# VectorE's order beside the late tile of a fused attention and mixture-of-experts kernel

## The chip, the cores and the metric

The kernel runs on one core of one Trainium2 chip. The metric is device time of one execution in microseconds (us), the median of the runs shown. TensorE is called PE here, VectorE DVE, ScalarE ACT, GpSimd POOL and SyncE SP, as in the profile.

## The reference

A linear attention with a decay per head makes 3072 tokens of 512 features; a router of two levels sends each to one of 16 experts; the expert is two matrix products with a ReLU between them, scaled by the router's weight.

```python
for t in range(S):                       # 4 batches, 8 heads, S = 768, D = 64
    state = gamma * state + k_t v_t^T
    y[:, :, t] = scale * q_t state
x = y as [3072, 512]
g = argmax(x @ w_group); e = argmax(x @ w_expert[g])       # 4 x 4 experts
h = np.maximum(xg[mask_e] @ w1[g, e], 0.0)                 # 512 -> 1024
ye = h @ w2[g, e]                                          # 1024 -> 512
out[tok_idx] = combined[:, None] * ye
```

## The kernel before, in words

**Stages.** Attention runs over 12 steps (up to some 104 us of the trace), and the routing of finished tokens runs beside it in batches. Then come the experts. Expert 0 is taken as two tiles: an early one of 128 tokens known from the first 16 chunks (`ua`), and a **late tile** of up to 108 tokens (`ub`), whose tokens are known only when the last batch is routed. Then comes expert 1 (`va`, up to 236 tokens), and then the other 14, from the one with most tokens to the one with fewest (`us[1:]`).

**Precision.** Each product of fp32 matrices is three products of 16-bit parts. The weights are split into a high part `wh` (ACT, L751) and a low part `wl` (DVE, L753), in 8 pieces of 128x1024 per expert. The tokens' rows are gathered by POOL (L775), transposed on PE into a PSUM tile `tpx` (L793), and split into high rows `xbh` (ACT, L795) and low rows `xbl` (DVE, L818). The hidden values are split out of PSUM into `hh` (ACT, L845) and `hl` (DVE, L848; for the early tile L1323 and L1330, since they are held back).

**The two layers of a tile.** `layers` is a generator. The first product has four groups `f2`, each two half blocks of 12 matmuls (L841); it yields after every half block. The second product of the late tile is `narrow`: 8 steps `k` of 12 matmuls (L947), with a yield after each. So the late tile's loop over `i` has 16 turns, 0 to 7 in the first product, 8 to 15 in the second. What is written into the loop at turn `i` is queued, on whatever engine it runs, behind what the generator queued before that yield. The order on every engine is that of the program: nothing is moved by a scheduler.

**What the late tile carries beside it.** On DVE: the ranking of the experts by their number of tokens (`order`, 9 steps, L597 to L626), which ends in the table `ord` that SP reads to choose the next experts' weights; `own_counts` (L583, L585), which makes `ocols`, the numbers of columns in expert 1's two tiles; six low pieces of expert 1's weights; and `counts` (L639 to L645), which makes `cols`, the same numbers for the later experts. On PE, `shape` reads such a number into a register of PE's queue (L806, a load that waits for DVE) and sets a matmul shape with it (L807): for `ocols` behind the late tile's steps k=1 and k=2, for `cols` behind the second group f2 of expert 1 and the third. On SP: two reads of `ord`, the lists of two experts (L768), and the loads of the next expert's weights (L725), each of which waits for a low piece that frees its buffer.

**Ahead of it**, the last batch's routing chooses experts (DVE to L403), PE makes the ranks (L436, L438), and DVE turns them into the late tile's token numbers (L555 and L567, with matmuls L563 between). Half blocks of the early tile are laid between these steps by `first(n)`.

Of the kernel before, what the change touches and what calls it, by code (L numbers as in the profile page):

```python
# [106 lines left out]
class Kernel:  # L107
# [1098 lines left out]
    def run(self):  # L1206
        tc, nc = self.tc, self.nc
        with ExitStack() as ctx:
# [18 lines left out]
            us = [dict(at=((j + 1) % 2, 0), W=(PW[-1:] + WIDTH)[j], pool=wpool[(j + 1) % 2]) for j in range(NS + 1)]  # L1227
            va = us[0]
# [4 lines left out]
            def pick(j):  # L1233
                self.picked(us[j], j - 1)

            def cols(j, i):
                return self.cols[0:1, i, j - 1:j] if j else self.own[:, i:i + 1]

            def first(n):

                for _ in range(n):
                    next(self.first, None)
# [65 lines left out]
            late.append(self.late_entries(5, self.oh[:, 0:BM, 0:1]))  # L1308
            self.route_steps(99, True)
            assert not self.steps  # L1310
            first(3)
            self.wsplit(va, 2, low=False)
            next(route)
            while next(route) != "late":
# [8 lines left out]
                nc.vector.scalar_tensor_tensor(*h)  # L1323
            for _ in route:
                pass
            first(2)
            p, y = self.at
            ent = self.entries(5, *self.chosen(y, self.yp))
            self.spreads.append((self.marks(p, self.yp), ent))
# [2 lines left out]
            nc.gpsimd.memset(self.xg[1], 0.0)  # L1332
            self.wsplit(va, 3, low=False)
            self.steps.append(self.order())
            self.route_steps(5)
            for i, k in enumerate(self.first):
                if i == 0:
                    self.wsplit(va, 4, low=False)
# [5 lines left out]
                if i == 3:  # L1344
# [3 lines left out]
                    self.nc.vector.tensor_copy(ub["mt"][:, 0, 1:2], self.final[:, 0, 1, 1:2])  # L1348
                    va["mt"] = self.final[:, 1]
                    self.gather(va)  # L1350
            self.route_steps(99)
            assert not self.steps
            pick(1)
            pick(2)
            for u in us[1:3]:
                self.listed(u)
            self.own_counts()
            self.wsplit(va, 0, high=False)
            ub["wh"], ub["wl"] = ua["wh"], ua["wl"]
            self.gather(us[1])  # L1360
            for i, k in enumerate(self.layers(ub)):
                if i in (1, 3):
                    self.wsplit(va, 6 + i // 2, low=False)
                if i in (8, 12):
                    self.xtrans(va, ("sta", "big")[i // 4 - 2], (i // 4 - 2,))
                if i in (3, 7, 12, 13, 14):
                    low = (3, 7, 12, 13, 14).index(i) + 1
                    self.wsplit(va, low, high=False)
                    if low % 2:
                        self.wload(us[1], low // 2)  # L1370
                if i in (9, 10):
                    self.shape(va, 0, i - 9, cols(0, i - 9))
                if i == 15:
                    self.counts()
# [83 lines left out]
```

## Time and profile before

| what | us |
|---|---|
| median of 3 runs (lowest, highest) | 406.8 (406.68, 407.85) |
| the profiled execution, its own time | 405.67 |
| its span, first to last instruction | 403.9 |
| PE busy, share of the span | 389.8, 97% |
| DVE busy, share of the span | 295.3, 73% |
| ACT busy, share of the span | 223.0, 55% |
| POOL busy, share of the span | 166.8, 41% |

The span is 1.8 us shorter than the execution's own time, which also holds what lies before the first and behind the last instruction. Busy shares are averages over stages with different limits, so the profile has to be read by stretches: which engine has idle time in a stretch, and what that idle time ends with. A matmul's row lasts longer than its distance to the next one, since matmuls are pipelined; time lost by PE is read from starts.

### The profile page before, as it was taken

The page shows a single profiled execution, that of the slowest core. Times are in us where ns is not written, and L with a number is a line of the kernel's source. Part 1 is how long each engine was busy: PE and PEld are TensorE (multiplying, and loading weights), DVE is VectorE, ACT ScalarE, POOL GpSimd, SP SyncE. Part 2 cuts the span into 40 slices and gives each one's busy share as a digit, 9 for nine tenths or more (in the row PEclk, how much of TensorE's full clock was granted, in tenths as well). Part 3 has the DMA queues.
Part 4 walks back from the last instruction along what each step waited for, and adds up shares of the span by engine and source line. Part 5 has one row for each costly group of instructions (what it writes and reads, how often), then busy time and mean ns, then how long its engine had stood idle before and what let it go on. Part 6 is the DMA issues. An engine that isn't in the chain of part 4 may idle for free.

```text
span 403.9 us, 13857 instructions
## 1 busy us (share of the span) xinstructions
PE 389.8 (97%) x5809; PEld 324.4 (80%) x5841; DVE 295.3 (73%) x483; ACT 223.0 (55%) x340; POOL 166.8 (41%) x172
## 2 busy tenths in 40 slices
PE   9999999999998999999999999999999999999992
PEld 5789888888858878586978888797887978879792
DVE  4575876868798879886758686776878769788620
ACT  3224434544652765565566666676666767667520
POOL 4542769659585106131416234260522505232001
PEclk9999999999999999999999999999999999999997
DMA  7999999988816897887868787979789897887001
GB/s 254 356 346 346 317 355 292 355 283 290 288 69 208 304 363 263 264 262 246 252 228 267 258 298 262 299 276 320 260 282 330 274 325 268 256 333 278 11 32 36
DMA packets 38643, 107.13 MB, mean 265 GB/s; under 512 B 12020, under 2 KB 12148, under 8 KB 31156
## 3 DMA queue, kind: packets, MB, share of 16 engines
q1 hardware_dynamic: 28752, 92.52, 67.0%
q0 software_dynamic: 9536, 12.63, 8.9%
q10 hardware_dynamic: 292, 1.08, 0.8%
q8 instruction: 47, 0.77, 0.7%
q14 instruction: 16, 0.13, 0.1%
HBM read 94.18 MB, written 13.20 MB: 266 GB/s over the span
## 4 chain that ended last, share of the span: by engine, by line
PE 46%; issue 36%; POOL 10%; DVE 4%; ACT 1%; DMA 1%; POOLq 0%; SPq 0%; ACTq 0%; DVEq 0%
PE hps L841 12%; POOL out L999 6%; PE op L299 5%; PE yps L875 5%; PE sh L235 5%; POOL xg L775 4%; PE op L286 3%; PE yps L922 3%; PE sh L345 2%; PE stp L261 2%; PE yps L925 2%; PE sh L319 1%; PE sh L220 1%; PE log L332 1%; PE tpx L793 1%
## 5 line engine op out<-in xcount | busy, mean ns | idle before, releaser
L753 DVE TENSOR_TENSOR wl<-wf,wh 128x1024 bf16<-128x1024 f32 x120 | 145.1, 1220 | 36.9 <-ACT wh L751 33.0
L751 ACT ACTIVATE wh<-wf 128x1024 f16<-128x1024 f32 (+1 forms) x136 | 133.6, 1001 | 0.1
L841 PE MATMUL hps<-xbl,wh 128*128 128x128 f16 (+16 forms) x544 | 128.4, 249 | 0.7 <-issue 0.5
L841 PE MATMUL hps<-xbh,wh 128*128 128x0 bf16 x544 | 125.9, 241 | 0.3 <-issue 0.3
L841 PE MATMUL hps<-xbh,wl 128*128 128x0 bf16 x544 | 125.9, 241 | 0.2 <-issue 0.2
L999 POOL DMA_INDIRECT out<-yo,mt x30 | 39.1, 1303 | 159.0 <-ACT yo L981 121.1
L841 PEld LDWEIGHTS <-wh 128*128 128x128 f16 x1088 | 94.9, 98 | 1.5 <-issue 0.9
L925 PEld LDWEIGHTS <-wh 128*128 128x128 f16 x768 | 47.1, 97 | 22.9
L845 ACT ACTIVATE hh<-hps 128x256 bf16<-128x256 f32 (+16 forms) x68 | 34.1, 503 | 43.6 <-PE hps L841 41.6
L775 POOL DMA_INDIRECT xg<-xd,mt x30 | 51.8, 1727 | 13.1 <-issue 5.2
L841 PEld LDWEIGHTS <-wl 128*128 128x128 bf16 x544 | 53.1, 98 | 1.6 <-issue 0.9
L247 DVE TENSOR_TENSOR pf<-sh,tri 128x512 f32<-128x512 f32 x48 | 30.6, 685 | 22.7 <-PE op L299 8.3
L795 ACT ACTIVATE xbh<-tpx 128x512 bf16<-128x512 f32 (+14 forms) x32 | 16.7, 523 | 45.9 <-PE tpx L793 45.9
L848 DVE SCALAR_TENSOR_TENSOR hl<-hps,hh 128x216 f16<-128x216 f32 (+15 forms) x64 | 36.6, 574 | 4.2 <-ACT hh L845 3.7
L922 PE MATMUL yps<-wh,hh 128*128 128x512 f16 x96 | 36.4, 379 | 0.0
L922 PE MATMUL yps<-wh,hl 128*128 128x512 f16 x96 | 36.4, 379 | 0.0
L922 PE MATMUL yps<-wl,hh 128*128 128x512 bf16 x96 | 36.3, 378 | 0.0
L818 DVE TENSOR_TENSOR xbl<-tpx,xbh 128x512 f16<-128x512 f32 (+14 forms) x32 | 19.1, 597 | 20.0 <-ACT xbh L795 20.0
L925 PEld LDWEIGHTS <-wl 128*128 128x128 bf16 x384 | 24.2, 97 | 11.4
L192 POOL TENSOR_TENSOR vs<-lv,cst 128x512 f32<-128x512 f32 x24 | 24.6, 1043 | 14.9 <-DMA lv<-qkv 9.9
L925 PE MATMUL yps<-hl,wh 128*128 128x108 f16 (+11 forms) x384 | 29.1, 198 | 0.0
L925 PE MATMUL yps<-hh,wh 128*128 128x0 bf16 x384 | 26.6, 190 | 0.0
(194 smaller groups left out, 599.1 us busy)
## 6 DMA issues: line engine op xcount, KB each, us to landing
wf<-w2p SPq DMA_DIRECT2D x29, 1024.0 KB
wf<-w1p SPq DMA_DIRECT2D x28, 1024.0 KB
lq<-qkv SPq DMA_DIRECT2D x24, 256.0 KB
lk<-qkv SPq DMA_DIRECT2D x24, 256.0 KB
lv<-qkv SPq DMA_DIRECT2D x24, 256.0 KB
xd<-xr SPq DMA_DIRECT2D x22, 256.0 KB
wf<-w1p SPq DMA_DIRECT2D x16, 256.0 KB
wf<-w2p SPq DMA_DIRECT2D x8, 256.0 KB
```

The lines of the kernel that those rows point to most:

```text
L192: self.nc.gpsimd.tensor_tensor(o, v, g, ALU.mult)
L235: nc.tensor.matmul(self.sh[2 * u + par][64 * half:64 * half + 64, cs], kT[rs, ks:ks + 64], qT[rs, cs], start=True, stop=True, skip_group_c ...
L247: nc.vector.tensor_tensor(o, sc, tri, ALU.mult)
L751: nc.scalar.activation(u["wh"][i][:, cs], u["wf"][i][:, cs], AF.Copy)
L753: (eng or nc.vector).tensor_tensor(u["wl"][i][:, cs], u["wf"][i][:, cs], u["wh"][i][:, cs], ALU.subtract)
L775: nc.gpsimd.indirect_dma_start(out=xg[0:r, i, :], out_offset=None, in_=self.xd[0:n, :], in_offset=bass.IndirectOffsetOnAxis(ap=mt[0:r, i, ...
L841: nc.tensor.matmul(o, l[:, k, fs], m, start=(n == 0), stop=(n == 11), skip_group_check=True)
L845: nc.scalar.activation(hh[:, f, 0:W], hv[:, :, 0:W], AF.Relu)
L848: nc.vector.scalar_tensor_tensor(*rest)
L922: nc.tensor.matmul(big, h[:, k, 0:P], w[k], start=(n == 0), stop=(n == 23))
L925: nc.tensor.matmul(o, w[k][:, d * P:d * P + P], m, start=(n == 0 and d == 0), stop=(n == 23), skip_group_check=True,)
L999: s = nc.gpsimd.indirect_dma_start(out=self.out, out_offset=bass.IndirectOffsetOnAxis(ap=mt[0:r, i, 0:1].bitcast(U32), axis=0), in_=yo[0:r ...
```

## The change

DVE's work beside the late tile is put in another order, and one half block of the early tile is moved ahead of the ranks. No instruction is added or removed.

```diff
-            first(3)
+            first(4)
             self.wsplit(va, 2, low=False)
...
-            first(2)
+            first(1)
...
             self.steps.append(self.order())
-            self.route_steps(5)
+            self.route_steps(3)
...
-            self.route_steps(99)
-            assert not self.steps
-            pick(1)
-            pick(2)
-            for u in us[1:3]:
-                self.listed(u)
-            self.own_counts()
-            self.wsplit(va, 0, high=False)
+            self.route_steps(2)
             ub["wh"], ub["wl"] = ua["wh"], ua["wl"]
-            self.gather(us[1])
             for i, k in enumerate(self.layers(ub)):
...
-                if i in (3, 7, 12, 13, 14):
-                    low = (3, 7, 12, 13, 14).index(i) + 1
+                if i == 1:
+                    self.wsplit(va, 0, high=False)
+                if i == 3:
+                    self.route_steps(2)
+                if i == 7:
+                    self.route_steps(99)
+                    assert not self.steps
+                    pick(1)
+                    pick(2)
+                    for u in us[1:3]:
+                        self.listed(u)
+                    self.own_counts()
+                if i == 10:
+                    self.gather(us[1])
+                if i in (7, 12, 13, 14, 15):
+                    low = (7, 12, 13, 14, 15).index(i) + 1
                     self.wsplit(va, low, high=False)
```

On DVE, from the ranking's fourth step on, before (the number behind a name is its buffer; hh_2385 and hps_2387, 2417, 2448, 2475 are the late tile's, wl_1931 is expert 1's first two low pieces):

```order
L607 TENSOR_TENSOR gt_2262<-key_2258 128x256
L612 TENSOR_REDUCE pos_2264<-gt_2262 128x16
L818 TENSOR_TENSOR xbl_2303<-tpx_2304,xbh_2302 128x4x108
L529 TENSOR_TENSOR lists_129<-lists_129,tally_2322 128x160
L534 SCALAR_TENSOR_TENSOR final_2025<-lists_129 128x32
L535 TENSOR_REDUCE final_2025<-lists_129 128x32
L1348 COPY mt_2192<-final_2025 128x1
L615 TENSOR_TENSOR eq_2341<-pos_2264,rest_94 128x256
L620 TENSOR_TENSOR eqk_2343<-eq_2341,rest_94 128x256
L623 TENSOR_REDUCE ordf_2345<-eqk_2343 128x16
L626 CAST ord_2347<-ordf_2345 128x16
L583 TENSOR_TENSOR ofc_2374<-nb_2137,rest_94 1x2
```

On DVE, the same stretch now:

```order
L818 TENSOR_TENSOR xbl_2299<-tpx_2300,xbh_2298 128x4x108
L529 TENSOR_TENSOR lists_129<-lists_129,tally_2318 128x160
L534 SCALAR_TENSOR_TENSOR final_2025<-lists_129 128x32
L535 TENSOR_REDUCE final_2025<-lists_129 128x32
L1348 COPY mt_2205<-final_2025 128x1
L607 TENSOR_TENSOR gt_2337<-key_2258 128x256
L612 TENSOR_REDUCE pos_2339<-gt_2337 128x16
L848 SCALAR_TENSOR_TENSOR hl_2342<-hps_2343,hh_2341 128x2x108
L753 TENSOR_TENSOR wl_1931<-wf_1752,wh_1930 128x1024
L848 SCALAR_TENSOR_TENSOR hl_2342<-hps_2374,hh_2341 128x2x108
L615 TENSOR_TENSOR eq_2402<-pos_2339,rest_94 128x256
L620 TENSOR_TENSOR eqk_2404<-eq_2402,rest_94 128x256
```

The late tile's low rows (L818) stand ahead of the ranking, and the low parts of h (L848) come between its steps.

On DVE, the rest of the late tile, before (wl_2129 and wl_2274 are expert 1's low pieces 2 to 5, xbl_2518 its low rows):

```order
L585 TENSOR_SCALAR ocols_2373<-ofc_2374 1x1 x2
L753 TENSOR_TENSOR wl_1931<-wf_1752,wh_1930 128x1024
L848 SCALAR_TENSOR_TENSOR hl_2386<-hps_2387,hh_2385 128x2x108
L848 SCALAR_TENSOR_TENSOR hl_2386<-hps_2417,hh_2385 128x2x108
L753 TENSOR_TENSOR wl_1931<-wf_1752,wh_1930 128x1024
L848 SCALAR_TENSOR_TENSOR hl_2386<-hps_2448,hh_2385 128x2x108
L848 SCALAR_TENSOR_TENSOR hl_2386<-hps_2475,hh_2385 128x2x108
L753 TENSOR_TENSOR wl_2129<-wf_1813,wh_2128 128x1024
L818 TENSOR_TENSOR xbl_2518<-tpx_2519,xbh_2517 128x4x128
L818 TENSOR_TENSOR xbl_2518<-tpx_2600,xbh_2517 128x4x108
L753 TENSOR_TENSOR wl_2129<-wf_1813,wh_2128 128x1024
L753 TENSOR_TENSOR wl_2274<-wf_2011,wh_2273 128x1024 x2
```

On DVE, the rest of the late tile now:

```order
L848 SCALAR_TENSOR_TENSOR hl_2342<-hps_2406,hh_2341 128x2x108
L848 SCALAR_TENSOR_TENSOR hl_2342<-hps_2433,hh_2341 128x2x108
L623 TENSOR_REDUCE ordf_2460<-eqk_2404 128x16
L626 CAST ord_2462<-ordf_2460 128x16
L583 TENSOR_TENSOR ofc_2489<-nb_2150,rest_94 1x2
L585 TENSOR_SCALAR ocols_2488<-ofc_2489 1x1 x2
L753 TENSOR_TENSOR wl_1931<-wf_1752,wh_1930 128x1024
L818 TENSOR_TENSOR xbl_2511<-tpx_2512,xbh_2510 128x4x128
L818 TENSOR_TENSOR xbl_2511<-tpx_2599,xbh_2510 128x4x108
L753 TENSOR_TENSOR wl_2142<-wf_1813,wh_2141 128x1024 x2
L753 TENSOR_TENSOR wl_2270<-wf_2011,wh_2269 128x1024 x2
L639 TENSOR_TENSOR eqc_2651<-eq_2402,cnt_2256 128x256
```

The order of experts and `ocols` (L623 to L585) stand behind all four low parts of h, and four low pieces instead of three stand between expert 1's last low rows and `counts` (L639, which before follows the last row shown). On PE, POOL and SP the order is the same as before, but for the one half block on PE.

## Rows read from the trace of the kernel before

**Rows 1.** Busy time by stretches: us, then busy time (and instructions) of PE, PEld, DVE, ACT, POOL

```profile
134.42:390.00 255.58, 255.58 (x3110) 209.36 (x3136) 197.92 (x233) 162.91 (x224) 81.58 (x53) 1.00 0.77 264
```

**Rows 2.** Timeline of PE: start us, us, what [idle before <-releaser]

```profile
106.49 0.22 PE L841 MATMUL hps<-xbh,wl 128*128 128x0 bf16 x1
107.05 0.20 PE L436 MATMUL log<-oh,stri 128*128 128x80 bf16 x1 [0.34 <-ACT ex L409]
...
115.05 0.50 PE L793 MATMUL tpx<-ident,xg 108*128 108x108 f32 x3 [0.21 <-DVE hl L1330]
...
116.77 0.72 PE L522 MATMUL tally<-yT,hot 128*128 128x160 bf16 x8
...
117.59 0.20 PE L841 MATMUL hps<-xbh,wl 128*128 128x0 bf16 x1
118.00 0.30 PE L841 MATMUL hps<-xbl,wh 128*128 128x108 f16 x3 [0.21 <-DVE xbl L818]
...
120.65 0.20 PE L841 MATMUL hps<-xbh,wh 128*128 128x0 bf16 x1 [0.27 <-issue]
...
121.39 0.21 PE L841 MATMUL hps<-xbl,wh 128*128 128x108 f16 x1 [0.50 <-issue]
...
125.10 0.28 PE L947 MATMUL yps<-hh,wh 128*128 128x0 bf16 x3 [0.23 <-issue]
...
134.52 0.26 PE L841 MATMUL hps<-xbl,wh 128*128 128x236 f16 x1
```

**Rows 3.** Timeline of DVE around the late tile

```profile
112.02 2.04 DVE L494 TENSOR_TENSOR yT<-rest,tile 128x128 bf16<-128x128 f32 x1
...
114.58 0.41 DVE L1330 SCALAR_TENSOR_TENSOR hl<-hps,hh 128x256 f16<-128x256 f32 x1
...
115.45 1.53 DVE L607 TENSOR_TENSOR gt<-key 128x256 f32<-128x256 f32 x1
...
117.35 0.59 DVE L818 TENSOR_TENSOR xbl<-tpx,xbh 128x432 f16<-128x432 f32 x1
117.86 0.31 DVE L529 TENSOR_TENSOR lists<-lists,tally 128x160 f32<-128x160 f32 x1
...
118.69 0.42 DVE L615 TENSOR_TENSOR eq<-pos,rest 128x256 f32<-128x256 f32 x1
...
120.66 1.20 DVE L753 TENSOR_TENSOR wl<-wf,wh 128x1024 bf16<-128x1024 f32 x1
121.79 0.65 DVE L848 SCALAR_TENSOR_TENSOR hl<-hps,hh 128x216 f16<-128x216 f32 x2
...
127.76 3.48 DVE L753 TENSOR_TENSOR wl<-wf,wh 128x1024 bf16<-128x1024 f32 x3
131.16 0.41 DVE L639 TENSOR_TENSOR eqc<-eq,cnt 128x256 f32<-128x256 f32 x1
...
132.28 0.17 DVE L645 TENSOR_SCALAR cols<-cols 128x14 int32<-128x14 int32 x1
```

**Rows 4.** Timeline of POOL beside these

```profile
112.61 1.28 POOL L501 TENSOR_TENSOR yT<-yT,pc 128x640 bf16<-128x640 bf16 x1
...
115.43 1.27 POOL L501 TENSOR_TENSOR yT<-yT,pc 128x640 bf16<-128x640 bf16 x1
```

**Rows 5.** Timeline of ACT and of SP's queue

```profile
115.67 0.53 ACT L795 ACTIVATE xbh<-tpx 128x432 bf16<-128x432 f32 x1 [1.47 <-PE tpx L793]
...
121.56 0.35 ACT L845 ACTIVATE hh<-hps 128x216 bf16<-128x216 f32 x1 [1.03 <-remote]
...
124.39 5.07 SPq L725 DMA_DIRECT2D wf<-w1p  x2
```

**Rows 6.** Tile ocols, and line 806 at 132 to 134: ns min/median/max, first and last start us

```profile
L806 PEldq TENSOR_LOAD <-ocols x2: 302/306/311, 123.2 to 124.2; - x2
...
L806 PEldq TENSOR_LOAD <-cols x1: 299/299/299, 132.9 to 132.9; - x1
```

**Rows 7.** Timeline of PE's weight loads, where the shape from cols is set

```profile
133.68 0.06 PEld L807 MOVE_SHAPE   x1
```

## The prediction

> **What bounds the kernel now.** First the busy time by stretches [rows 1]: from 134.42 us, where expert 1's third group begins, to 390, PE is busy 255.58 of 255.58 us. Nothing that another engine does there can end earlier than PE. So the change is worth what it moves the start of that stretch, the matmul at 134.52 [rows 2], and nothing else, as long as the later stretch stays closed. Second, the timeline of PE before it [rows 2], read for its idle marks. There are five that bear on this change: 0.34 us before the ranks (waiting for ACT's `ex`), 0.21 before the late tile's transposes (waiting for DVE's held-back `hl`, L1330), 0.21 before the late tile's first product with low rows (waiting for L818), 0.27 and 0.50 at 120.65 and 121.39 ("issue": the profile shows no wait). Third, the timelines of DVE [rows 3] and POOL [rows 4], to see what DVE does just ahead of each of these waits. Fourth, PE's own reads of shapes [rows 6], since they wait for DVE and everything on PE's queue stands behind them. The gap at 125.10 [rows 2] belongs to them: the second read of `ocols` starts at 124.2 [rows 6] and takes 0.30, and the register steps behind it some 0.6 more, which is known from the third read, of `cols`: it starts at 132.9 [rows 6] and its shape is set from 133.68 to 133.74 [rows 7], 0.84 in all.
>
> **Part 1, the ranks half a block later.** The four half blocks ahead of the ranks now hold the matmuls that filled PE's time after the token numbers. Between the starts at 106.49 and 107.05 [rows 2] PE does nothing but a matmul of 0.055 us (128 columns, the first group's pitch), so 0.5 is lost. Twelve such matmuls are 0.65 us, so the ranks come some 0.15 later, the token numbers (L567) with them, and PE is 0.5 ahead behind them. That lead ends at the transposes at 115.05, which wait for L1330 at 114.58 to 114.99 [rows 2, 3]: PE only waits there longer. Is L1330 then 0.15 later? By DVE's rows alone, yes, since DVE has no idle from L567 to it: the sum has +0.15. But L494 ahead of it lasts 2.04 [rows 3] and ends at 114.06, just behind POOL's L501, 112.61 to 113.89 [rows 4]. The Trainium skill says (SBUF — State Buffer, Who interferes with whom) that a DVE instruction with two SBUF inputs and a GpSimd instruction that reads SBUF exclude each other, and the first to start holds the port to its end; by that L494 ends with L501 whenever it starts, and the term would be 0. The sum takes 0, since 114.06 follows 113.89 by 0.17, and L607 shows the same: 115.45 to 116.98 beside the second L501, 115.43 to 116.70 [rows 3, 4]. Bounds: 0 and +0.15.
>
> **Part 2, the low rows ahead of the ranking.** Now L818 waits for L607 (1.53) and L612 and starts at 117.35. The high rows are ready at 115.67 + 0.53 = 116.20 [rows 5]. With nothing ahead of it, L818 runs from 116.26 to about 116.85; were it held by L501 to 116.70, to 117.3. Both are before 117.59, where PE first lacks low rows [rows 2]. The step from 117.59 to 118.00 falls to the pitch of 0.04: **-0.37**.
>
> **Part 3, what is late instead.** The tally's matmuls end at 116.77 + 0.72 = 117.49 [rows 2], so L529 starts at 117.5 instead of 117.86, and the four instructions up to L1348 end at 118.69 - 0.35 = 118.35 [rows 3]. From there DVE does, in order: L607 and L612 at 0.42 each, the duration of L615 of the same size, since no L501 runs now (0.84); one low part of h (0.33, half of the 0.65 at 121.79); a low piece (1.13, from 120.66 to 121.79); a low part (0.33); L615 and L620; two low parts (0.65); L623 to L585. L615 to L585 took 120.66 - 118.69 = 1.97. The sum is 5.25, so `ocols` is there at **123.6**, 2.9 later than now.
>
> PE reads it at 123.2 [rows 6], and with part 2 and without the two issue gaps it would come 0.37 + 0.77 earlier, at 122.1. So it waits, and steps k=2 to k=7 stand behind that read. The read starts 0.4 later than now, and so do the shapes, step k=3 (125.10), the transposes of expert 1's second tile, its low rows and the start of expert 1: **+0.4** where now nothing is lost. What PE gains before is given back here, whether the issue gaps vanish or not, unless they make `ocols` later (below).
>
> Behind expert 1's low rows DVE has four low pieces instead of three. Now L753 x3 and `counts` run from 127.76 to 132.28 + 0.17 = 132.45; then 0.4 + 1.13 later, at 133.98. PE's read of `cols` now starts at 132.9, 0.45 behind it; then it starts at 133.98 and the first matmul of group three 0.84 + 0.06 later, at 134.88, against 134.52: +0.36. Counted along PE instead, with the waits between 125.10 and 134.52 unchanged, it is +0.4. Two ways, nearly one number: **+0.4** at 134.52.
>
> **Part 4, at nothing.** The table `ord` is ready 2.9 later, so SP's two lists and its first weight load move from 124.39 to 127.3 [rows 5], and POOL's gathers of expert `us[1]`, which wait for those lists, by as much; nothing on SP or POOL changes places with them. Cover: ACT takes that load's data first at about 133.1 now, 8.7 after its issue; 5.8 are left for 1 MB. The gathered rows are transposed at about 141. Were this cover gone, ACT's split and the `hh` behind it would wait, and PE's second product at 139. The low pieces 1 to 3 are finished over 3 us before expert 1's groups use them. The scatter of the late tile's rows (POOL) stands behind those gathers and is waited for by none.
>
> **Sum:** -0.5 (gone at the transposes) and -0.37 on PE (given back at the read of `ocols`), and +0.4 from that read: 405.67 + 0.4 = 406.1 in the profiled execution, which is 1.1 under the median of the runs. On the median, 406.8 + 0.4 = **407.2**. A change of 0.3% (1.2 us) is what a measurement of this kernel can tell from none.
>
> **Rivals.**
> *The late part of h (slower).* The gaps at 120.65 and 121.39 are unexplained, and ACT's second `hh` of the late tile starts only at 121.56, 1.03 idle before it [rows 5]. The sum lets it start at 120.2 with the gaps. DVE now stands behind it with its low part, and behind that with the whole ranking. It decides from 120.65, when the first low piece is done. If that stall stays where it is, 0.37 earlier, `hh` ends at 121.54 and DVE goes on with 0.33, then L615 and L620 (0.92), 0.65, and 1.05: 124.5, which is 0.9 later than in the sum. The end is +1.3: **408.1**. For it: the second `hh` was late although DVE and ACT were not in its way, so this change doesn't remove its cause. Against: PE's pace into that place changes, and nothing ties a gap to it. Chance 0.27.
> *PE is not held (faster).* If the read of `ocols` is no wait, because DVE is through by about 122.2 (it would be if L494 took not 2.04 but about what L501's hold leaves out, and the transposes and the tally came earlier by what DVE gains), then the 0.37 and the 0.77 are kept, 1.14 in all, and the read of `cols` comes as early as it must: **405.6** to 405.7. For it: L494 is late by chance of POOL's order. Against: that order is not changed, and the transposes can gain no more than PE's own lead of 0.5 and the 0.21 there, half of the 1.4 that is wanted. Chance 0.15.
> *It is all hidden.* The added wait at `ocols` equals what PE gained, within 0.2: 406.8. This falls in the forecast's range. Chance 0.1 of the forecast's 0.58.
>
> **How the numbers follow.** Forecast 0.58 (406.5 to 407.7, with the +0.15 of part 1 and the half microsecond between runs), the slower rival 0.27 (407.9 to 408.5), the faster 0.15 (405.2 to 405.9). 0.3% is 405.6 and 408.0. Half of the faster rival's range lies under 405.6, and a closed PE stretch that fits better adds a little: 0.13. Slower takes most of the second case and the forecast's upper tail: 0.27. Same: 0.60. The range reaches to both rivals' middle: 405.8 to 408.5.
>
> **What would show it.** Right: L607 at about 0.42 and behind L1348; L818 done before 117.3 and no idle mark before the first product with `xbl`; `ocols` at 123.6, PE's read of it there, with an idle stretch of PE before k=2; group three of expert 1 at 134.9. Wrong: PE's read of `ocols` earlier than 122.5 (the faster rival), or a second low part of h later than 121.2 (the slower one), or idle marks of PE behind 135, which would mean that part 4's cover is gone.

## The result, and the profile after

The changed kernel takes 409.63 us (median of 7 runs) against 406.8 (7 runs): a ratio of 1.0068, 95% interval 1.0040 to 1.0095, so it is slower by some 2.8 us (1.6 to 3.9 by the interval). The forecast was 407.2, its range ended at 408.5. In the tables below the medians are over all runs, while the ratios leave out the few executions that ran in a slower state, the profiled one of e17 among them. The profiled execution of the changed kernel took 406.89 (span 405.2) and is the shortest of the seven; in it the attention part ended 0.87 us earlier than in the profile of before (DVE's choice of experts, L403, at 105.57 and at 106.44). So places in the two traces are compared by their distance from a common point: the start of the late tile's transposes (L793), 115.05 before [rows 2] and 114.24 after. From there to expert 1's third group it is 134.52 - 115.05 = 19.47 us before and 135.60 - 114.24 = 21.36 after: 1.9 more. That is inside the interval; what the medians differ by beyond it stands in no trace (see e1).

Timeline of PE after the change (start us, us, what, idle before it and its releaser), the rows that answer to [rows 2]:

```profile
114.24 0.56 PE L793 MATMUL tpx<-ident,xg 108*128 108x108 f32 x4 [0.89 <-DVE cnt L597]
...
118.43 0.20 PE L841 MATMUL hps<-xbh,wl 128*128 128x0 bf16 x1
...
119.88 0.20 PE L841 MATMUL hps<-xbh,wh 128*128 128x0 bf16 x1 [0.42 <-issue]
...
120.61 0.20 PE L841 MATMUL hps<-xbh,wl 128*128 128x0 bf16 x1 [0.41 <-issue]
...
121.33 0.21 PE L841 MATMUL hps<-xbh,wh 128*128 128x0 bf16 x1 [0.34 <-issue]
...
125.34 0.31 PE L947 MATMUL yps<-hh,wh 128*128 128x0 bf16 x4 [1.44 <-DVE ocols L585]
...
126.30 0.31 PE L947 MATMUL yps<-hh,wh 128*128 128x0 bf16 x4 [0.30 <-issue]
...
135.60 0.26 PE L841 MATMUL hps<-xbl,wh 128*128 128x236 f16 x1 [1.01 <-DVE hl L848]
```

The idle mark before the first product with low rows is gone, as forecast. The issue gaps are not: there are three now, 1.17 us of idle time, where there were two with 0.77. Then come two waits that the kernel before does not have: 1.44 us for `ocols` at step k=2, and 1.01 before group three. The second is written to DVE's L848; it ends with `cols`, as the reads show: the first of them starts at 134.6, just behind L644 (134.40 to 134.57 in DVE's timeline below), which makes the first row of `cols`.

Tile `ocols`, and line 806 at 133 to 137 (ns min/median/max, first and last start):

```profile
L806 PEldq TENSOR_LOAD <-ocols x2: 304/305/306, 124.4 to 125.4; - x2
```

```profile
L806 PEldq TENSOR_LOAD <-cols x2: 300/302/305, 134.6 to 136.2; - x2
```

One wait between groups of expert 1, for ACT's `yT` (L953), became shorter; it is 1.16 in the first of these rows, from PE before, and 0.25 in the second, from PE after:

```profile
131.86 0.65 PE L994 MATMUL tpy<-ident,yT 128*108 128x128 f32 x4 [1.16 <-ACT yT L953]
```

```profile
131.76 0.65 PE L994 MATMUL tpy<-ident,yT 128*108 128x128 f32 x4 [0.25 <-ACT yT L953]
```

Timeline of DVE after the change, which answers to [rows 3]:

```profile
111.12 2.03 DVE L494 TENSOR_TENSOR yT<-rest,tile 128x128 bf16<-128x128 f32 x1
...
115.40 0.61 DVE L818 TENSOR_TENSOR xbl<-tpx,xbh 128x432 f16<-128x432 f32 x1 [0.88 <-ACT xbh L795]
...
117.53 0.41 DVE L607 TENSOR_TENSOR gt<-key 128x256 f32<-128x256 f32 x1
...
118.61 1.22 DVE L753 TENSOR_TENSOR wl<-wf,wh 128x1024 bf16<-128x1024 f32 x1
121.78 0.38 DVE L848 SCALAR_TENSOR_TENSOR hl<-hps,hh 128x216 f16<-128x216 f32 x1 [1.96 <-ACT hh L845]
...
124.26 0.20 DVE L585 TENSOR_SCALAR ocols<-ofc 1x1 int32<-1x1 f32 x2
...
128.96 4.62 DVE L753 TENSOR_TENSOR wl<-wf,wh 128x1024 bf16<-128x1024 f32 x4
133.50 0.42 DVE L639 TENSOR_TENSOR eqc<-eq,cnt 128x256 f32<-128x256 f32 x1
...
134.40 0.17 DVE L644 SCALAR_TENSOR_TENSOR cols<-num,rest 128x14 int32<-128x14 f32 x1
134.61 0.20 DVE L645 TENSOR_SCALAR cols<-cols 128x14 int32<-128x14 int32 x1
```

POOL's L501 beside L494, which answers to [rows 4]:

```profile
111.71 1.28 POOL L501 TENSOR_TENSOR yT<-yT,pc 128x640 bf16<-128x640 bf16 x1
```

DVE sits idle for 1.96 us ahead of the second low part of h, with the ranking and `ocols` behind it. It waits for ACT's second `hh`, and ACT's row names PE as what it waits for; the timeline of ACT, which answers to [rows 5]:

```profile
117.72 0.35 ACT L845 ACTIVATE hh<-hps 128x216 bf16<-128x216 f32 x1 [0.90 <-PE hps L841]
...
121.39 0.35 ACT L845 ACTIVATE hh<-hps 128x216 bf16<-128x216 f32 x1 [2.38 <-PE hps L841]
```

The second `hh` starts 3.67 behind the first; before it was 121.56 - 119.24 = 2.32. The rows of before that this rests on, from ACT and from PE:

```profile
119.24 0.35 ACT L845 ACTIVATE hh<-hps 128x216 bf16<-128x216 f32 x1 [1.58 <-PE hps L841]
```

```profile
119.64 0.20 PE L841 MATMUL hps<-xbh,wl 128*128 128x0 bf16 x1
```

This matmul at 119.64, and the one at 118.43 after the change, is the 48th of the late tile, the last that the second `hh` needs. So by PE's rows the second `hh` comes 1.92 us behind its matmuls before and 2.96 after, and each time just behind the start that ends the last issue gap (121.39 before, 121.33 after; 0.05 to 0.17 us behind it in all ten profiles with gaps). In a profile without gaps (e15) it is 0.44. The idle time of the gaps lies behind these matmuls, so the rows do not show what holds the second `hh`; gaps and late `hh` only come together.

Behind group three the expert stretch is closed as it was (windows; the columns of [rows 1]), 254.40 busy of 254.40 us:

```profile
135.60:390.00 254.40, 254.40 (x3097) 208.31 (x3125) 197.41 (x233) 161.97 (x223) 82.00 (x53) 1.00 0.78 268
```

So the 1.9 us are lost between the late tile's transposes and group three, where PE waits at two reads of shapes. That was the place the prediction named. What was open is how much each costs, and why the second `hh` came still later.

### The profile page after: what moved, and what is told of

It is laid out like the page before. It is cut to its first block, busy times and chain, and to the rows that moved or that the text cites. A ratio compares the mean times of both kernels' runs of the same rounds, so it can differ in the third digit from the quotient of the medians.

```text
span 405.2 us, 13857 instructions
## 1 busy us (share of the span) xinstructions
PE 390.8 (96%) x5809; PEld 325.0 (80%) x5841; DVE 293.3 (72%) x483; ACT 223.2 (55%) x340; POOL 166.2 (41%) x172
## 4 chain that ended last, share of the span: by engine, by line
PE 47%; issue 35%; POOL 10%; DVE 5%; ACT 1%; POOLq 0%; DVEq 0%; ACTq 0%
PE hps L841 11%; POOL out L999 6%; PE yps L875 5%; PE op L299 5%; PE sh L235 5%; POOL xg L775 4%; PE op L286 3%; PE sh L345 3%; PE yps L922 3%; PE stp L261 2%; PE yps L925 2%; DVE wl L753 1%; PE log L332 1%; PE sh L319 1%; PE sh L220 1%
## 5 line engine op out<-in xcount | busy, mean ns | idle before, releaser
L753 DVE TENSOR_TENSOR wl<-wf,wh 128x1024 bf16<-128x1024 f32 x120 | 145.1, 1220 | 35.7 <-ACT wh L751 34.5
L848 DVE SCALAR_TENSOR_TENSOR hl<-hps,hh 128x216 f16<-128x216 f32 (+15 forms) x64 | 36.7, 574 | 6.0 <-ACT hh L845 5.6
L818 DVE TENSOR_TENSOR xbl<-tpx,xbh 128x512 f16<-128x512 f32 (+14 forms) x32 | 19.1, 597 | 22.0 <-ACT xbh L795 22.0
```

The source lines that it names most:

```text
L753: (eng or nc.vector).tensor_tensor(u["wl"][i][:, cs], u["wf"][i][:, cs], u["wh"][i][:, cs], ALU.subtract)
L848: nc.vector.scalar_tensor_tensor(*rest)
```

## The experiments

Each set of runs was taken on one chip, with runs of the kernel before beside it; the sets e1 to e18 came to five different chips (the chip of the first result is not on record). That turned out to matter: **in some sets PE has the issue gaps beside the late tile in every profile, in others in none.** Below, "chips with the gaps" stands for the chips of such sets; no chip was used for two sets, so a chip and the time of its set are not told apart.

The first table gives the times. The ratio and its interval are those on record; the ratio is not the quotient of the two medians and differs from it by up to 0.2%. The kernel before against itself (e9) gives 1.0009, with 0.27% to either side. So differences of 0.2 to 0.3% are at the edge of what can be told, and such readings below rest on the distances in the traces too.

| run | median, us | before in its set | ratio to before (95%) | issue gaps |
|---|---|---|---|---|
| e1 the change | 409.07 | 407.14 | 1.0064 (1.0034, 1.0094) | yes |
| e2 change, `ocols` early | 406.92 | 407.14 | 1.0016 (0.9991, 1.0040) | yes |
| e3 before, ranks alone | 406.90 | 407.14 | 1.0014 (0.9986, 1.0041) | yes |
| e4 before, low rows alone | 406.60 | 407.14 | 1.0002 (0.9970, 1.0033) | yes |
| e5 change, `ocols` and `cols` early | 404.40 | 405.15 | 0.9981 (0.9952, 1.0010) | no |
| e6 before, low rows, `cols` early | 404.39 | 405.15 | 0.9972 (0.9945, 0.9999) | no |
| e7 change, gather later | 406.59 | 405.15 | 1.0030 (0.9995, 1.0064) | no |
| e8 change, fixed shape | 407.17 | 405.15 | 1.0055 (1.0026, 1.0085) | no |
| e9 before | 407.39 | 406.87 | 1.0009 (0.9982, 1.0036) | yes |
| e10 the change | 408.44 | 406.87 | 1.0044 (1.0016, 1.0073) | yes |
| e11 before, `ocols` late | 408.00 | 406.87 | 1.0016 (0.9992, 1.0040) | yes |
| e12 before, low pieces shifted | 407.27 | 406.87 | 1.0007 (0.9975, 1.0038) | yes |
| e13 as e5 | 404.18 | 405.56 | 0.9974 (0.9948, 0.9999) | no |
| e14 as e6 | 404.80 | 405.56 | 0.9981 (0.9958, 1.0004) | no |
| e15 the change | 405.80 | 405.56 | 1.0024 (0.9996, 1.0051) | no |
| e16 as e12 | 406.30 | 405.56 | 1.0023 (0.9996, 1.0050) | no |
| e17 as e5 | 404.73 | 405.82 | 0.9960 (0.9929, 0.9990) | no |
| e18 before, one run | 404.37 | 405.82 | | no |

The second table gives distances on PE in the profiled executions, from the late tile's transposes (T) to its second product (Y), to expert 1's first matmul (E) and to its third group (G). The distances are free of where the attention part happened to end.

| profile | gaps | T to Y | Y to E | E to G | T to G |
|---|---|---|---|---|---|
| before | yes | 7.70 | 5.21 | 6.56 | 19.47 |
| the change | yes | 8.04 | 6.88 | 6.44 | 21.36 |
| e10 the change | yes | 8.10 | 7.02 | 6.44 | 21.56 |
| e2 `ocols` early | yes | 8.12 | 5.22 | 6.34 | 19.68 |
| e4 low rows alone | yes | 8.30 | 5.25 | 5.22 | 18.77 |
| e18 before | no | 7.16 | 6.09 | 5.22 | 18.47 |
| e15 the change | no | 6.22 | 7.32 | 6.36 | 19.90 |
| e16 low pieces shifted | no | 6.22 | 7.30 | 6.35 | 19.87 |
| e13 `ocols`, `cols` early | no | 6.22 | 6.89 | 4.79 | 17.90 |

**e1, the change again.**

> The changed kernel once more, for a second profile and more times. The theory: the loss is made in the stretch from the late tile's first product to expert 1's third group, by two waits of PE that the kernel before does not have: the read of ocols (1.44 us idle in the first profile of the change) and the read of cols (1.01). It expects both again within 0.3, ACT's second hh of the late tile again at 121 or later, PE closed from group three on, and 409.6 in the median. The rival, that the first profile's waits belong to that one execution (which was the shortest of seven) and the others lose their time elsewhere, expects under 0.7 at either read and idle marks of PE in another stretch.

T to G is 21.48; 1.48 us idle at `ocols`, 0.97 before group three, the second `hh` 3.79 behind the first. The theory's waits are there again. This set also has the mean granted clock of PE for each run. Six of the twelve runs of the change are under 0.993 (median 409.65 us, the others 408.31), and five of the 33 of the kernel before that the ratio uses (408.02, the others 406.51). Among the runs at 0.993 or more the change loses 1.8 us, and in the set of e10 1.6 (408.17 against 406.60), near the 1.9 to 2.0 of the distances. So most of the loss stands where the clock is the same. That more of the change's runs have a lower clock can account for the rest of its median; why they have it is not shown.

**e2, `ocols` alone early.** Now DVE makes it where it is idle, before the late tile.

```diff
             self.route_steps(3)
+            self.own_counts()
...
                         self.listed(u)
-                    self.own_counts()
```

> The change, with own_counts alone put back ahead of the late tile, so that ocols is ready at about 118 while ranking, low rows and low pieces stay as the change has them. The theory (PE waits at ocols because it stands behind the late second hh): PE's 1.44 us of idle time before step k=2 go, expert 1's rows and with them cols come as much earlier, and the time falls by 1.2 to 1.5 to about 408.2; what is left over the kernel before is the wait at cols, with four low pieces ahead of it. First rival (cols is bound by DVE's sum of work alone, not by PE's rows): the wait at ocols goes but the one at cols grows by as much, 409.5. Second rival (the ranks' half block or something outside the late tile costs the time): no idle at ocols and no gain, 409.6.

Timeline of PE:

```profile
123.92 0.32 PE L947 MATMUL yps<-hh,wh 128*128 128x0 bf16 x4 [0.24 <-issue]
...
133.13 0.26 PE L841 MATMUL hps<-xbl,wh 128*128 128x236 f16 x1 [1.39 <-DVE hl L848]
```

The wait at `ocols` is gone, Y to E is back at 5.22, and T to G at 19.68. The time falls from 409.07 to 406.92 in the same set, by more than the theory said: nearly the whole loss goes with this one read (T to G 21.48 to 19.68, before 19.47). The three issue gaps and the late second `hh` are unchanged. So against the kernel before, which has two gaps, the third one and the later `hh` cost little by themselves; they cost through what stands behind them on DVE. What the gaps cost against none this run does not tell: the kernel before has 19.47 with them and 18.47 without (e18).

**e3, ranks alone** (the two `first` lines of the change, on the kernel before).

> The kernel before with only the first part of the change: the ranks half a block later. The theory, as the prediction had it: 0.5 us are gained at the ranks and lost again at the late tile's transposes, which wait for the held-back low part of h: 406.8, within 0.2. The rival that the change's loss comes from here: 409 or more. A second rival (the token numbers come 0.15 later and everything behind them): 407.0.

T to G is 19.49, and the transposes wait 0.96 where they waited 0.21: the half microsecond gained at the ranks is lost there, as forecast.

**e4, low rows alone** (`route_steps(5)` to `route_steps(3)`, on the kernel before).

> The kernel before with only the second part: the late tile's low rows ahead of the last half of the ranking, which still ends ahead of the late tile, as do ocols and the first low pieces. The theory: PE's idle mark of 0.21 before the first product with low rows goes (0.37 from start to start), ocols is late by under 0.3 and is waited for by none, so 406.4 to 406.8. The rival that PE's pace at the late tile's issue gaps sets the end, whatever comes before: 406.8. The rival that putting the low rows first is itself what costs the time: 408 or more.

The first idle mark is gone, but T to Y is 8.30 against 7.70: the issue gaps are three, as in the change, and take more than the low rows give. T to G is nevertheless 18.77, because the wait of 1.16 that the kernel before has between groups of expert 1, for ACT's `yT` (L953), is not there. `ocols` stands 0.54 later behind L403 (under 0.3 was expected), and none waits for it. In the median no difference can be told.

**e5 and e6, both reads freed.** e5 is e2 with `counts` ahead of the four low pieces; e6 is e4 with `counts` ahead of the last of three.

```diff
+                    if i == 12:
+                        self.counts()
                     self.wsplit(va, low, high=False)
...
-                if i == 15:
-                    self.counts()
```

> The change with own_counts ahead of the late tile, and with counts (which makes cols) ahead of the first of the four low pieces instead of behind the fourth. The theory (what is left of the loss is PE's wait at cols, 1.39 us idle before group three in the run with own_counts early, and it comes from four low pieces ahead of counts): the idle mark before group three goes, group three stands about 27.0 behind the last choice of experts (L403) instead of 28.3, and the time falls to 405.4 to 405.8, under the kernel before. The rival (PE is then held by the late tile's second hh or by expert 1's h instead, since the four low pieces still stand between them on DVE): a new wait of 0.7 or more before group three or four, 406.5 or more.

> The kernel before with the low rows ahead of the ranking and counts one low piece earlier. The theory, by which the end is set by PE's two reads: the idle mark of 0.25 before group three in the run with the low rows alone goes (0.4 from start to start), group three stands 27.1 behind L403 instead of 27.5, 406.0 to 406.3. The rival that something else of PE holds it there: 406.6, as with the low rows alone.

No idle mark is left before group three in either (T to G 17.83 and 18.41), and both come out under the kernel before, though e5's interval includes no difference. But this set's profiles show no issue gaps at all, and the second `hh` 1.2 behind the first, although e6 has the same work in the same order as e4 up to `counts`. So DVE's order does not by itself make the gaps; the changed kernel itself has none in e15.

**e7 and e8, what the gaps hang on.** e7 moves `self.gather(va)` into the late tile's turn 5; e8 takes out the line that sets the late tile's shape, so that its matmuls run over all 108 columns.

> The change with POOL's gather of expert 1's rows issued half a product later, behind the late tile's sixth half block; the rows are transposed later by that, so the time itself is not comparable. It asks what PE's issue gaps of the late tile (three, 1.2 us idle in all) and the late second hh hang on. If on the gather's transfers: the gaps move with it, by 2 us or more, or go, and the second hh starts within 1.5 of the first plus the weight split. If on PE's own pace: gaps and second hh stand where they do in the change, 3.7 behind the first hh.

> The change without the shape that PE sets for the late tile, so that its matmuls run over all 108 columns. If PE's issue gaps and the late second hh hang on the dynamic shape, the gaps go and the second hh comes 1.5 us or more earlier; then ocols comes 1 us earlier, PE's wait there falls from 1.4 to about 0.4 and the time by about 1, less what the wider matmuls cost (at most 0.01 each, some 2 us over 192). If not: the gaps stay within 0.5 of 1.2 us in all.

Both ran in the set without gaps, so neither can tell: inconclusive. They do show that the change's second wait needs no gaps: 1.39 and 1.26 idle before group three, though there the gathered rows of expert 1 are late too (1.62 and 1.66 us of waiting for them). e8 has no wait at `ocols` and still loses 0.55%, part of which its wider matmuls take (T to Y 6.85 against 6.22).

**e9 and e10, both kernels beside each other.**

> The kernel before once more. PE's issue gaps beside the late tile (1.0 us idle or more, with the second hh 2.3 to 3.8 behind the first) stand in the six profiles taken so far in the first two sets, and in none of the four of the third set. If they belong to the set of executions (the chip they ran on) and not to the kernel, this profile has them or not as its neighbours here have. Without them the theory expects PE at the late tile to be held by the gathered rows of expert 1 (an idle mark before the transposes of step k=0) and group three about 27.5 behind L403; with them 28.1. The rival, that the gaps are the kernel's: as in the first profile, 0.27 and 0.50.

> The changed kernel beside the one before, on the same chip. The first theory (ocols stands behind the late second hh, so that the whole loss hangs on PE's issue gaps): where the gaps are absent, ocols is at 0.9 us earlier against L403, its read waits under 0.5, and the loss falls to under 1 us. The second theory (two waits of DVE's making, the second of them at cols behind four low pieces, which needs no issue gap): the idle mark before group three is 1.0 to 1.4 and the loss stays 1.5 to 2.5 whether the gaps are there or not.

This chip has the gaps, with the kernel before too. T to G is 19.62 for the kernel before and 21.56 for the change: a loss of 1.9, and 1.8 by the ratio, as the second theory says for such a chip. What the first says of a chip without gaps is answered by e15. The waits of the change in PE's timeline:

```profile
126.12 0.31 PE L947 MATMUL yps<-hh,wh 128*128 128x0 bf16 x4 [1.59 <-DVE ocols L585]
...
136.38 0.26 PE L841 MATMUL hps<-xbl,wh 128*128 128x236 f16 x1 [1.01 <-DVE hl L848]
```

**e11, the mirror of e2:** the kernel before, with `own_counts` alone moved to the late tile's turn 7.

> The kernel before with own_counts alone moved behind the late tile's four low parts of h; ranking, low rows and low pieces as before. DVE then makes ocols at about 124.4 in the time of the first profile (123.51 + 0.65 + 0.3) instead of 120.7. The theory: PE's second read of late shapes waits for it, 0.5 to 1.2 us idle at step k=2, and with three low pieces the wait at cols does not follow in full: 0.4 to 1.0 us slower than before. The rival (PE has slack there, from expert 1's gathered rows): no more than 0.2.

PE waits 1.13 us for `ocols` at step k=2, and T to G is 21.76, 2.1 over e9. In the median it is 1.1 us, by the ratio 0.65, and the interval includes no difference. The profile shows a second loss that the theory had not: 0.81 us before expert 1's first matmul, for its low rows. And the issue gaps are three (two in the kernel before), with no other change of order ahead of them. What makes two or three of them is open.

**e12 and e16, the low pieces' places alone.**

```diff
-            self.wsplit(va, 0, high=False)
...
-                if i in (3, 7, 12, 13, 14):
+                if i == 1:
+                    self.wsplit(va, 0, high=False)
+                if i in (7, 12, 13, 14, 15):
```

> The kernel before with only the positions of expert 1's low pieces taken from the change: the first one behind the late tile's first half of f2=0, four instead of three between expert 1's low rows and counts. Ranking, low rows and ocols as before. The theory (the second wait, at cols, is one low piece of 1.13 us on DVE's chain): an idle mark of 0.7 to 1.3 before group three, 0.6 to 1.1 slower than before. The rival (what delays cols in the change is PE's late arrival alone): no idle mark there, within 0.2 of before.

> The kernel before with only the low pieces' positions of the change. The theory: cols is made 1.1 later on DVE. Where PE waits 1.2 us or more for ACT's yT ahead of group three, as in the kernel before on chips with gaps, that wait covers it and the time is that of before within 0.2%; where it doesn't, an idle mark of 0.7 to 1.3 before group three and 0.2 to 0.3% over before.

With gaps (e12) the time is that of before, 1.0007; its profiled execution had PE at a lower clock for three microseconds (last section), so its distances from T on are not used. Behind that stretch the expected idle mark before group three is there (1.25 us), but the time that should have followed from it (0.6 to 1.1 more) is not: the wait for ACT's `yT`, 1.16 in the kernel before, is gone in its place. Without gaps (e16) it loses 0.23%, as much as the whole change beside it (e15, 0.24%), though either interval just reaches no difference. The timelines of DVE and of PE in e16:

```profile
129.47 4.62 DVE L753 TENSOR_TENSOR wl<-wf,wh 128x1024 bf16<-128x1024 f32 x4
```

```profile
136.02 0.26 PE L841 MATMUL hps<-xbl,wh 128*128 128x236 f16 x1 [1.39 <-DVE hl L848]
```

Four pieces, and the read waits.

**e13 to e18, the rest.**

> The change with own_counts ahead of the late tile and counts ahead of the four low pieces, on another chip if it comes so. The theory (the two waits of PE at ocols and cols are the whole loss): no idle mark over 0.4 at either read, group three 26.4 to 27.2 behind L403, and no slower than the kernel before, 0.1 to 0.3% under it, with PE's issue gaps or without. The rival (what was gained belongs to the chip without the gaps): with gaps 0.2% or more over the kernel before.

> The kernel before with the low rows ahead of the ranking and counts one low piece earlier. The theory: no idle mark at the read of cols, group three 27.1 to 27.3 behind L403, 0.1 to 0.3% under the kernel before, with the gaps or without. The rival: with gaps no different from before.

> The changed kernel. With PE's issue gaps: as in its three profiles, idle 1.4 to 1.6 at the read of ocols and 1.0 at cols, group three 30.0 to 30.3 behind L403, 0.4 to 0.7% over before. Without them: no wait at ocols (PE waits for the gathered rows one step before), 1.2 to 1.4 at cols, group three 28.5 to 29, 0.2 to 0.4% over before.

> The change with own_counts ahead of the late tile and counts ahead of the four low pieces. With PE's issue gaps the theory expects group three about 27.1 behind L403 (28.31 in the run with own_counts early, less its wait at cols of 1.2) and 0.1 to 0.4% under the kernel before; without them 26.4 to 27.1 and 0.1 to 0.3% under. The rival: with gaps no different from before.

> The kernel before. Without PE's issue gaps: held by the gathered rows at step k=0 (0.6 us idle or more), group three 27.1 to 27.6 behind L403. With them: as in its two profiles, 28.1.

Neither set has gaps, so none of these runs tells what e13, e14 and e17 expected for a chip with them. The change there (e15), PE:

```profile
123.19 0.63 PE L793 MATMUL tpx<-ident,xg 128*128 128x128 f32 x4 [1.75 <-DMA xg<-xd,final]
...
134.45 0.26 PE L841 MATMUL hps<-xbl,wh 128*128 128x236 f16 x1 [1.40 <-DVE hl L848]
```

The kernel before there (e18), PE:

```profile
123.04 0.63 PE L793 MATMUL tpx<-ident,xg 128*128 128x128 f32 x4 [0.58 <-DMA xg<-xd,final]
...
133.11 0.26 PE L841 MATMUL hps<-xbl,wh 128*128 128x236 f16 x1 [0.25 <-PE hps L841]
```

Without the gaps the change does gain at the first product (T to Y 6.22 against 7.16), and loses it one step later, where PE now waits 1.75 instead of 0.58 for the gathered rows of expert 1. `ocols` is done at 122.6, before that wait ends, and costs nothing, as the first theory of e10 says. What remains is the wait at `cols`, the second theory's: E to G is 6.36 against 5.22, or 1.14, one low piece (L753, 4.62 / 4 = 1.16). In e13 it is gone: DVE makes `cols` ahead of the pieces.

```profile
128.56 0.24 DVE L645 TENSOR_SCALAR cols<-cols 128x14 int32<-128x14 int32 x1
128.64 4.63 DVE L753 TENSOR_TENSOR wl<-wf,wh 128x1024 bf16<-128x1024 f32 x4
```

E to G is 4.79 there, and PE is closed from 124.78 on (windows):

```profile
124.78:390.00 265.22, 265.21 (x3285) 218.80 (x3314) 204.43 (x243) 166.42 (x230) 88.76 (x57) 1.00 0.77 266
```

This order (e5, e13, e17: the change with `ocols` ahead of the late tile and `cols` ahead of the four pieces) has been under the kernel before in all three of its sets, by 0.19, 0.26 and 0.40%, in two of them with an interval that excludes no difference; e6 and e14 by 0.28 and 0.19%. All of these were on chips without the gaps. Whether they beat the kernel before where the gaps are was not measured; e2, which still has its wait at `cols`, was equal to it there. The profile of e17 cannot be used for distances behind L403 (group three 30.1 behind it, 26.4 to 27.1 expected): the late tile's rows came late in that execution (last section).

## Why the prediction was wrong

- **What bounds the kernel** held: the expert stretch stayed closed, and the change was worth what it did to the start of group three.
- **Part 1** held. The lead from the ranks ended at the transposes, and its term of 0 with bounds 0 and +0.15 holds: the transposes start 8.67 behind L403 in the change and 8.74 in e3, against 8.61 before and 8.57 in e9, and e3 has T to G at 19.49 against 19.47. L494 ended behind L501 again (113.15 and 112.99). The reason given for the term is shown only in part. The Trainium skill (SBUF — State Buffer, Who interferes with whom) says that a DVE instruction with two SBUF inputs contends with a GpSimd instruction that reads SBUF, and that issue order decides who blocks. The trace agrees with the first, since L494 lasts until L501 has ended. It does not show the second: by the rows L494 starts 0.59 ahead of L501 (111.12 and 111.71 here, 112.02 and 112.61 before) and is the one that is held.
- **Part 2** was right in its place and useless in its effect. L818 ran at 115.40 to 116.01 and the idle mark went. But the -0.37 was to be given back at `ocols`; on chips with gaps it had gone before that, into a third issue gap (T to Y 8.04, 8.10 and 8.30 in the profiles with early low rows, 7.70 before). On chips without gaps it was given back at the gathered rows, a wait that the trace of before did not show.
- **Part 3, `ocols` at 123.6, is the step that failed.** The sum put `ocols` 123.6 - 106.44 = 17.16 behind L403, with the second `hh` at 120.2, early enough not to hold DVE, since the gaps were to vanish. Where they are absent it stands at 17.3 (e15): the sum of DVE's work was right. Where they are present, and they were present in the very trace that was read, it stands at 18.89 (124.46 - 105.57), 18.96 (e1) and 19.08 (e10). The argument that failed is "PE's pace into that place changes, and nothing ties a gap to it". The pace changed and the gaps stayed, and grew. The slower rival had this mechanism and its place, but with a chance of 0.27 only, and it had that stall where it "stays where it is": 124.5 - 106.44 = 18.06. `ocols` came 0.8 later than that, and the second `hh` 1.1 later than the rival had it (15.82 behind L403 against 121.19 - 106.44 = 14.75). So the +0.4 at the read is 1.67 (Y to E 6.88 against 5.21); with 0.34 more from T to Y and 0.12 less from E to G the loss is 1.9.
- **The read of `cols`**, +0.36 to +0.4, was right about the cause (a fourth low piece) and rests on a path that did not hold. "With the waits between 125.10 and 134.52 unchanged" is where it was missed: one of these waits, 1.16 at 131.86, fell to 0.25, and the new wait of 1.01 stands in its place (E to G 6.56 and 6.44 with gaps), so nothing is added to the first wait. Without gaps it is 1.14, since PE then has nothing else to wait for. `cols` came 1.7 later than forecast (134.81 - 105.57 = 29.24 behind L403 against 133.98 - 106.44 = 27.54), since the low rows of expert 1 ahead of it moved with the first wait. The count along DVE was also 0.2 too long, since the first read needs only L644 and not L645.
- **Part 4** held. PE has no idle mark behind group three, in the change as in e13, so neither the weights nor the gathered rows of the next expert were late.
- **The range** ended at 408.5, the upper end of the slower rival's own range (the prediction calls both ends the rivals' middle; that would be 408.2 and 405.55). The rival's condition, a stall with no known cause, was given one value, that of the one execution read. With the second `hh` where the three profiles of the change with gaps have it, 15.8 to 16.0 behind L403, 1.1 to 1.3 later than the rival's 14.75, the same rival gives 409 and more.

What stays open: what the issue gaps are, and with them why the second `hh` is late. In all profiles of three sets PE starts only one to five matmuls in 0.5 to 0.7 us, two or three times over, and ACT gets the matmuls before them late; in no profile of the three other sets. No releaser is shown, the granted clock reads 1.00 in that stretch, and the two runs meant to tell (e7, e8) met a chip without them.

## What to carry to other kernels

In this kernel a read of a matmul shape by PE's queue is a wait for everything behind it (1.4 to 1.6 us at `ocols`): put the few tiny instructions that make its value (here some 0.4 us in all) where the vector engine is idle, not behind work that waits for another engine. The idle marks with no releaser did not go with the new order, as the sum had assumed: price each path with such marks present, longer, and absent, and let the range hold what another chip may show. And where a stretch already has a wait, a second one did not add to it here until the first was gone.

## What the runs showed of the hardware that was not expected

**Which wait is on the path differed from set to set, and so, as far as is known, from chip to chip.** The kernel before took 407.1 and 406.9 us on two chips with the gaps and 405.2, 405.6 and 405.8 on three without. The change lost 0.64 and 0.44% on the former, through `ocols`, and 0.24% on the one of the latter where it ran, through `cols`; the interval of this last just reaches no difference.

**A DVE instruction of two elements took 2.1 us.** In the profiled execution of e17 POOL's gather of the late tile's rows came 1.75 us later than in the change's first profile (6.70 behind L403 against 4.95), and POOL's L501 with it; what it waited for the profile does not show. L583, which reads two tiles in SBUF, 1x2 elements each, took 2.11 us, to 117.22, instead of 0.14 (e4, e6); L501 ended at 117.20. The timelines of DVE and POOL:

```profile
115.11 2.11 DVE L583 TENSOR_TENSOR ofc<-nb,rest 1x2 f32<-1x2 f32 x1
```

```profile
115.92 1.28 POOL L501 TENSOR_TENSOR yT<-yT,pc 128x640 bf16<-128x640 bf16 x1
```

In the same way L597 (128x16) took 2.13 in e16, to 114.93, beside an L501 that ended at 114.89, and L423 (128x4) 2.14 in e4, to 113.01, with L501's end at 112.98. These three differ in size and last alike; in the trace of before L597 and L423 take 0.16. L818, whose first input is in PSUM, took 0.61 in the change (115.40) though L501 ran until 115.79. What holds the three is only in part shown: their ends follow L501's by 0.02 to 0.04, but by the rows each starts 0.81 to 0.83 ahead of L501, beside POOL's gather (in e17 114.72 to 115.88). And in e2, where L583 started at 113.61 and L501 at 113.71 with no gather just ahead, it took 0.14.

**PE's clock fell after a long wait, in two of the three profiles with the longest.** In the profiles of e12 and e17 the transposes waited 2.11 and 2.66 us for the late tile's gathered rows. The granted clock then fell from 1.00 to 0.50 (1.2 GHz) for some three microseconds, and the matmuls of 512 columns came every 0.43 us instead of 0.22. Windows of e12 (the columns of [rows 1]; the third figure from the end is the granted clock):

```profile
116.00:117.00 1.00, 0.00 (x0) 0.00 (x0) 0.96 (x2) 0.00 (x0) 0.92 (x3) 1.00 0.39 135
...
119.00:120.00 1.00, 1.00 (x4) 0.34 (x3) 0.61 (x1) 0.24 (x1) 0.98 (x2) 0.50 0.00 0
...
121.00:122.00 1.00, 1.00 (x20) 0.98 (x19) 0.21 (x1) 0.69 (x1) 0.00 (x0) 0.98 0.00 0
```

From the transposes to the tally it took 3.3 us instead of 1.7, and these two executions were among the longest of their kernels (411.39 and 409.36 against medians of 407.27 and 404.73). With a wait of 1.58 before the same transposes (e16) and of 1.46 (e15) the clock stayed at 1.00, but so it did in e7 with the longest of all, 2.90 us (transposes at 117.98); its window behind the wait:

```profile
118.00:119.00 1.00, 1.00 (x7) 0.67 (x8) 0.00 (x0) 0.42 (x1) 1.00 (x1) 1.00 0.00 0
```

So the length of the wait alone does not decide it, and what does is not shown. Where the clock fell, the wait cost some 1.6 us on top of its length. A lower mean clock goes with longer runs (e1 above), which is part of the scatter between runs of one kernel (404.16 to 409.58 us for the kernel before in the set of e1); where in those runs the clock fell is not recorded.
